# Rows of reciprocal norms: issued by ScalarE and spread over the partitions in one transfer

## The chip, the cores and the metric

The kernel runs on one core of a Trainium2 chip. The metric is the time of one execution on the device in microseconds (us), the median of several runs. The profile is of a single execution, whose span is a few microseconds shorter than the measured time. Everything is in float32.

## What is computed

Attention with normalised queries and keys, followed by a layer that works on a choice of the tokens only:

```
q, k, v: (8, 12, 448, 64);  g_q, g_k: (64)
q_n = q / sqrt(mean(q*q) + 1e-6) * g_q          (k_n likewise)
attn = softmax(q_n @ k_n.T / sqrt(64)) ;  x = attn @ v, as (8, 448, 768)
scores = x @ w_gate ;  the 128 tokens with the highest score of each of the 8 batches:
    out = x + sigmoid(score) * (relu(x @ w1) @ w2)      w1: 768x1024, w2: 1024x768
all other tokens: out = x
```

The part that matters here is the factor 1/rms of each query. It is one number per token and head, and the queries lie in memory transposed: head dimension on the partitions, tokens along the free dimension. So the factor has to be multiplied along the free dimension, with the same row of numbers on each of the 64 partitions of a head.

## The kernel before

The heads are taken in 24 groups of four (three groups to a batch). A group is a tile `qT` and a tile `kT` of 128 partitions (two heads of 64 dimensions) by 2 x 448 tokens, a tile `v`, and two tiles `tok` of 128 partitions by 896 numbers, which hold the same queries and keys with tokens on the partitions. From `tok` the squares are formed on ScalarE (`squares`, L207), their row sums on VectorE (`sum_squares`, L214), and the power -1/2 on GpSimd (L217), giving `rinv` of 128 partitions x 14 numbers.

For the keys, `rinv` is used as it lies, as the scale of the exponential (L298). For the queries it has to change its place. `rows_out` (L225) writes `rinv` to a small tensor `rows` in DRAM, 2 x 896 numbers, so that each pair of heads has its 1/rms in one contiguous row of 3584 bytes. `rows_in` (L233) reads each row back 64 times, onto 64 partitions, giving the tile `bc` (128 x 896). `scale_q` (L245) then multiplies `qT` by `bc` and by the product of both gains on VectorE (L248). Groups 0 and 1 don't take this way: `scale_q_early` spreads their rows by small matmuls.

A group is worked on in 7 units of 64 keys each. `scores` (L281) makes four pairs of matmuls into two PSUM banks (L289) and two exponentials on ScalarE (L298) that write a tile `p`; `values` (L306) multiplies `p` by `v` into two PSUM banks that stay for the whole group (L313); `add_probs` (L321) sums the `p` tiles on VectorE (L335). There are seven `p` buffers and four PSUM banks for scores. Later the sums become denominators (L367, L392, L394), the outputs are turned to tokens on rows (L410) and scaled (L412), and batch by batch the gate, the ranks, the selection by an indirect DMA, and the two layers (L575, L595) follow, in pieces put between the units.

The order is written out by hand: the program runs in manual order, each engine executes its instructions in the order in which the program issues them, and an engine that waits for a semaphore holds everything behind it. A table of slots says when each step is issued; slot u comes with unit u, and 168 units make the attention, s0 = 7n being the first slot of group n. Group n is prepared from slot `first` = max(s0 - 20, 0), or s0 - 17 for n up to 5: squares and sums in slots `first` to `first` + 3, then `rows_out` and `rows_in`; `scale_q` comes in slot max(s0 - 6, `first` + 11). Loads of `tok` are issued 26 slots ahead of s0, `qT` 13, `kT` and `v` 11. The weights w1 and w2 come in 14 parts, one every third slot from slot 16. All plain transfers, loads, rows and the stores of x (L424), are issued by SyncE, on one queue (q1 in the profile). Indirect transfers go by GpSimd (q0), and the queue of ScalarE (q10) carries one small transfer at the start. Each transfer signals its end by a semaphore. The transfers share eight of these, and an issue waits for the last user of the same one.

`bc` has two buffers, `rows` three, `qT` four, `kT` and `v` three each, `tok` six.

Of the kernel before, what the change touches and what calls it, by code (L numbers as in the profile page):

```python
# [68 lines left out]
def fast(  # L69
# [21 lines left out]
    nc = tc.nc  # L91

    B, NP, _, S = loads.src["qT"].shape
    CP = 112
    NJ = S // CP
    D = 64
# [59 lines left out]
    for c in range(2):  # L156
        nc.vector.memset(pick_pair[D * c : D * (c + 1), c : c + 1], 1.0)
    nc.vector.scalar_tensor_tensor(
        out=gg, in0=loads.gcol[:, 0:1], scalar=scale, in1=loads.gcol[:, 1:2], op0=OP.mult, op1=OP.mult
# [43 lines left out]
    def squares(n, i):  # L203
        t = get("tok", n, i)
        sq = sqs[(2 * n + i) % 2]
        for h in [slice(0, 1), slice(1, 2)] if (n, i) == (0, 0) else [slice(0, 2)]:
            nc.scalar.activation(out=sq[:, h, :, 0:D], in_=t[:, h], func=AF.Square, scale=scale)  # L207
        sss[n, i] = norm_pool.tile([128, 2, NI], F32, name="ss", bufs=4)
        return sq

    def sum_squares(n, i, sq):
        ss = sss.pop((n, i))
        for h in [slice(0, 1), slice(1, 2)] if (n, i) == (0, 0) else [slice(0, 2)]:
            nc.vector.tensor_reduce(out=ss[:, h], in_=sq[:, h], axis=AX.X, op=OP.add)  # L214
        rinv = norm_pool.tile([128, 2, NI], F32, name="rinv", bufs=8)
        flat = "p h i -> p (h i)"
        nc.gpsimd.tensor_tensor(  # L217
            out=rinv.rearrange(flat),
            in0=ss.rearrange(flat),
            in1=neg_half.to_broadcast([128, 2 * NI]),  # L220
            op=OP.pow,
        )
        rinvs[n, i] = rinv

    def rows_out(n):  # L225

        rows = dram_pool.tile([2, 2 * S], F32, name="rows", bufs=3)
        nc.sync.dma_start(
            out=rows.rearrange("h (p i) -> p h i", i=NI), in_=rinvs.pop((n, 0))
        )  # L230
        bcs[n] = rows

    def rows_in(n):  # L233

        rows = bcs[n]
        bc = norm_pool.tile([128, 2, S], F32, name="bc")
        for hh in range(2):
            src = rows[hh].rearrange("(c s) -> c s", c=2)
            nc.sync.dma_start(
                out=bc[D * hh : D * (hh + 1)],  # L240
                in_=dataclasses.replace(src, ap=[[0, D]] + [list(x) for x in src.ap]),
            )
        bcs[n] = bc

    def scale_q(n):  # L245
# [388 lines left out]
    def at(slot, fn, *args):  # L634
        todo.setdefault(slot, []).append(lambda: fn(*args))
# [22 lines left out]
    def prepare(n, slot):  # L658
        sq = {}
        for i in range(2):  # L660
            at(slot + 2 * i, lambda i=i: sq.setdefault(i, squares(n, i)))
            at(slot + 2 * i + 1, lambda i=i: sum_squares(n, i, sq.pop(i)))

        at(slot + (7 if n > 2 else 6), rows_out, n)
        at(slot + (10 if n > 5 else 9 if n > 2 else 8), rows_in, n)

    for n in range(1, n_groups):
        s0 = NI * n
        if n > 2:
            at(max(s0 - 26, 4 * (n - 3)), load, "tok", n, 0)  # L670
            at(max(s0 - 26, 4 * (n - 3)), load, "tok", n, 1)
        if n > 1:
            at(max(s0 - 13, 2), load, "qT", n)
            at(max(s0 - 11, 2), load, "kT", n)
            at(max(s0 - 11, 2), load, "v", n)
            first = max(s0 - (20 if n > 5 else 17), 0)
            prepare(n, first)
            at(max(s0 - 6, first + 11), scale_q, n)
# [666 lines left out]
```

## Time and profile before

| | |
|---|---|
| time, median of 3 runs | 531.6 us (530.16 to 532.11) |
| span of the profiled execution | 526.9 us, granted clock 0.994 |
| PE busy | 507.6 us |
| VectorE (DVE) busy | 334.2 us |
| ScalarE (ACT) busy | 278.1 us |
| GpSimd (POOL) busy | 191.8 us |
| DMA | 93.21 MB in 43405 packets |

The busy times are of instructions that compute. Issues of transfers and waits on semaphores are not counted in them; those of SyncE are found under SPq. "Idle before" and "waited for" name the event that released an engine last. A DMA share is the mean over the core's 16 DMA engines, and "us to landing" is counted from the issue to the arrival of the last byte.

### The profile page before, as it was taken

The page shows a single profiled execution, that of the slowest core. Times are in us where ns is not written, and L with a number is a line of the kernel's source. Part 1 is how long each engine was busy: PE and PEld are TensorE (multiplying, and loading weights), DVE is VectorE, ACT ScalarE, POOL GpSimd, SP SyncE. Part 2 cuts the span into 40 slices and gives each one's busy share as a digit, 9 for nine tenths or more (in the row PEclk, how much of TensorE's full clock was granted, in tenths as well). Part 3 has the DMA queues.
Part 4 walks back from the last instruction along what each step waited for, and adds up shares of the span by engine and source line. Part 5 has one row for each costly group of instructions (what it writes and reads, how often), then busy time and mean ns, then how long its engine had stood idle before and what let it go on. Part 6 is the DMA issues. An engine that isn't in the chain of part 4 may idle for free.

```text
span 526.9 us, 11121 instructions
## 1 busy us (share of the span) xinstructions
PE 507.6 (96%) x4482; PEld 298.8 (57%) x4482; DVE 334.2 (63%) x638; ACT 278.1 (53%) x507; POOL 191.8 (36%) x109
## 2 busy tenths in 40 slices
PE   6999997999999999999999999998999999999995
PEld 5544343565744476546654467644664448659694
DVE  4566879579846896658666787467947487336101
ACT  4886873857644845456644585645463474401100
POOL 4956866623512454132712424304621003002102
PEclk9999998999999999999999999999999999999998
DMA  8968779799764297526846396537542231104100
GB/s 304 382 217 291 244 224 345 251 291 340 200 187 161 82 291 232 163 94 192 260 136 183 87 297 211 159 103 223 195 131 71 70 136 31 31 1 143 53 32 35
DMA packets 43405, 93.21 MB, mean 177 GB/s; under 512 B 11059, under 2 KB 23348, under 8 KB 43346
## 3 DMA queue, kind: packets, MB, share of 16 engines
q1 hardware_dynamic: 39938, 86.11, 52.1%
q0 software_dynamic: 3264, 6.31, 3.5%
q8 instruction: 37, 0.61, 0.5%
q14 instruction: 22, 0.18, 0.1%
q10 hardware_dynamic: 144, 0.00, 0.0%
HBM read 74.93 MB, written 25.35 MB: 190 GB/s over the span
## 4 chain that ended last, share of the span: by engine, by line
PE 89%; DVE 4%; DMA 2%; ACT 2%; issue 2%; POOL 0%; DVEq 0%; SPq 0%; ACTq 0%; POOLq 0%
PE sc L289 24%; PE av L313 22%; PE moe_ps L575 13%; PE moe_ps L595 11%; PE sc L595 4%; PE x_ps L410 4%; PE sc L575 4%; PE den_ps L367 3%; DMA bc<-rows 2%; PE denT_ps L392 1%; ACT p L298 1%; DVE sum L335 1%; PE warm_ps L164 1%; DVE ss L214 1%; DVE x L412 1%
## 5 line engine op out<-in xcount | busy, mean ns | idle before, releaser
L298 ACT ACTIVATE p<-sc,rinv 128x448 f32<-128x448 f32 x336 | 186.6, 642 | 106.3 <-PE sc L289 92.5
L217 POOL TENSOR_TENSOR rinv<-ss,neg_half 128x14 f32<-128x14 f32 x48 | 128.8, 2689 | 198.3 <-DVE ss L214 170.6
L289 PE MATMUL sc<-qT,kT 64*64 64x448 f32 x1344 | 154.8, 549 | 1.1 <-DVE qT L268 0.4
L313 PE MATMUL av<-p,v 64*64 64x448 f32 x1344 | 147.1, 537 | 0.0
L335 DVE TENSOR_TENSOR sum<-sum,p 128x896 f32<-128x896 f32 x101 | 111.6, 1105 | 7.2 <-ACT p L298 0.9
L313 PEld LDWEIGHTS av<-p,v 64*64 64x64 f32 x1344 | 60.1, 133 | 67.6 <-issue 56.9
L289 PEld LDWEIGHTS sc<-qT,kT 64*64 64x64 f32 x1344 | 54.3, 133 | 70.9 <-issue 47.0
L214 DVE TENSOR_REDUCE ss<-sq 128x14 f32<-128x910 f32 (+1 forms) x49 | 52.4, 1074 | 33.9 <-ACT sq L207 33.9
L575 PE MATMUL moe_ps<-xeT,w 128*128 128x128 f32 x576 | 69.3, 277 | 0.0
L575 PEld LDWEIGHTS moe_ps<-xeT,w 128*128 128x128 f32 x576 | 66.2, 192 | 5.3 <-issue 5.3
L595 PE MATMUL moe_ps<-w,hT 128*128 128x384 f32 x176 | 61.3, 491 | 0.4 <-DVE xe L604 0.3
L412 DVE TENSOR_TENSOR x<-x_ps,rden 112x512 f32<-112x512 f32 x48 | 32.8, 690 | 37.2 <-PE x_ps L410 36.4
L506 POOL DMA_INDIRECT selected<-x,rank x32 | 33.6, 1050 | 47.3 <-DVE x L498 39.3
L207 ACT ACTIVATE sq<-tok 128x896 f32<-128x896 f32 (+1 forms) x49 | 46.4, 951 | 5.7 <-DMA tok<-in_tok_dram 3.7
L595 PEld LDWEIGHTS moe_ps<-w,hT 128*128 128x128 f32 x176 | 31.7, 190 | 22.5 <-issue 2.5
L436 DVE SCALAR_TENSOR_TENSOR prod<-x,wg 112x256 f32<-112x256 f32 x96 | 41.5, 432 | 3.0
L614 POOL DMA_INDIRECT out_dram<-xe,row x10 | 11.6, 1164 | 81.1 <-DVE rden L394 47.3
L410 PE MATMUL x_ps<-ident,xT 128*112 128x128 f32 x192 | 29.5, 279 | 3.3 <-DVE rden L394 3.3
L335 DVE TENSOR_TENSOR sum<-p 128x896 f32<-128x896 f32 x24 | 25.9, 1078 | 5.2 <-ACT p L298 5.2
L604 DVE SCALAR_TENSOR_TENSOR xe<-sc,xe 128x384 f32<-128x384 f32 (+1 forms) x6 | 3.3, 550 | 40.6 <-PE sc L595 40.6
L410 PEld LDWEIGHTS x_ps<-ident,xT 128*112 128x112 f32 x192 | 21.8, 135 | 12.6 <-issue 7.7
L248 DVE SCALAR_TENSOR_TENSOR qT<-qT,gg,bc 128x896 f32<-128x896 f32 x22 | 25.2, 1147 | 5.1 <-DMA bc<-rows 5.1
(71 smaller groups left out, 311.0 us busy)
## 6 DMA issues: line engine op xcount, KB each, us to landing
tok<-in_tok_dram SPq DMA_DIRECT2D x48, 448.0 KB, 6.3
qT<-in_qT_dram SPq DMA_DIRECT2D x24, 448.0 KB, 6.2
kT<-in_kT_dram SPq DMA_DIRECT2D x24, 448.0 KB, 7.0
v<-in_vp_dram SPq DMA_DIRECT2D x24, 448.0 KB, 7.7
out_dram<-x SPq DMA_DIRECT2D x8, 1344.0 KB, 7.8
bc<-rows SPq DMA_DIRECT2D x44, 224.0 KB, 6.4
xe<-selected SPq DMA_DIRECT2D x8, 385.0 KB, 3.1
w<-in_moe_w_dram SPq DMA_DIRECT2D x6, 512.0 KB, 6.4
```

What stands on the lines that cost most here:

```text
L207: nc.scalar.activation(out=sq[:, h, :, 0:D], in_=t[:, h], func=AF.Square, scale=scale)
L214: nc.vector.tensor_reduce(out=ss[:, h], in_=sq[:, h], axis=AX.X, op=OP.add)
L217: nc.gpsimd.tensor_tensor(out=rinv.rearrange(flat), in0=ss.rearrange(flat), in1=neg_half.to_broadcast([128, 2 * NI]), op=OP.pow,)
L289: nc.tensor.matmul(out=scs[hh][D * c : D * (c + 1), 0:S], lhsT=get("kT", n)[r, c, D * i : D * (i + 1)], rhs=get("qT", n)[r, c, :], start=True,
L298: nc.scalar.activation(out=p[:, hh], in_=scs[hh][:, 0:S], func=AF.Exp, scale=rinvs[n, 1][:, hh, i : i + 1],)
L313: nc.tensor.matmul(out=avs[n][c][D * hh : D * (hh + 1), 0:S], lhsT=get("v", n)[r, hh, i, :], rhs=probs[u][r, hh], start=(i == 0), stop=(i ...
L335: nc.vector.tensor_tensor(out=sums[n], in0=probs.pop(u - 1) if begins else sums[n], in1=probs.pop(u), op=OP.add)
L410: nc.tensor.transpose(out=ps[:CP, j, :], in_=t[:, j, :], identity=ident)
L412: nc.vector.tensor_tensor(out=xs[b][:, :, col : col + 128].rearrange("p j (h d) -> p j h d", d=D), in0=ps[:CP].rearrange("p j (h d) -> p j ...
L436: nc.vector.scalar_tensor_tensor(out=prod, in0=xs[b][:, j, cols], scalar=1.0, in1=wg[:, cols], op0=OP.mult, op1=OP.mult, accum_out=gates[b ...
L575: nc.tensor.matmul(out=ps[:, 128 * i : 128 * i + n], lhsT=w1[:, dc, 128 * (f0 + i) : 128 * (f0 + i + 1)], rhs=xeT[:, dc, :n], start=(dc == 0),
L595: nc.tensor.matmul(out=ps[:n, :width], lhsT=hT[:, fc, :n], rhs=w2[:, fc, cols], start=(fc == 0), stop=(fc == NFC - 1),)
```

## The change

`rows_out` and `rows_in` are issued on the queue of ScalarE instead of that of SyncE, so that they don't stand behind loads and stores that wait for their buffers. The spreading, two transfers of 64 partitions each, becomes one of 128 partitions, whose source is read as 2 rows, each 64 times, 896 numbers. And the two steps are put at fixed distances: `rows_out` in slot `first` + 6 and `rows_in` in slot `first` + 8, where they were one slot and one or two slots later for most groups.

```
     def rows_out(n):
         rows = dram_pool.tile([2, 2 * S], F32, name="rows", bufs=3)
-        nc.sync.dma_start(
+        nc.scalar.dma_start(
             out=rows.rearrange("h (p i) -> p h i", i=NI), in_=rinvs.pop((n, 0))
         )
...
         bc = norm_pool.tile([128, 2, S], F32, name="bc")
-        for hh in range(2):
-            src = rows[hh].rearrange("(c s) -> c s", c=2)
-            nc.sync.dma_start(
-                out=bc[D * hh : D * (hh + 1)],
-                in_=dataclasses.replace(src, ap=[[0, D]] + [list(x) for x in src.ap]),
-            )
+        (h_step, _), row = [list(x) for x in rows.ap]
+        nc.scalar.dma_start(
+            out=bc.rearrange("d c s -> d (c s)"),
+            in_=dataclasses.replace(rows[:, :], ap=[[h_step, 2], [0, D], row]),
+        )
...
-        at(slot + (7 if n > 2 else 6), rows_out, n)
-        at(slot + (10 if n > 5 else 9 if n > 2 else 8), rows_in, n)
+        at(slot + 6, rows_out, n)
+        at(slot + 8, rows_in, n)
```

The program's instructions on PE, VectorE and GpSimd stand in the same order as before. The lines of the changed kernel after these functions have numbers lower by one.

## Prediction

> **What bounds the kernel now.** I read the page top down (busy table, slices, chain, DMA issues), then the wait table, the view of the tile `bc`, and a table by stretches of time.
>
> ```profile
> PE 507.6 (96%) x4482; PEld 298.8 (57%) x4482; DVE 334.2 (63%) x638; ACT 278.1 (53%) x507; POOL 191.8 (36%) x109
> DMA  8968779799764297526846396537542231104100
> GB/s 304 382 217 291 244 224 345 251 291 340 200 187 161 82 291 232 163 94 192 260 136 183 87 297 211 159 103 223 195 131 71 70 136 31 31 1 143 53 32 35
> q1 hardware_dynamic: 39938, 86.11, 52.1%
> q10 hardware_dynamic: 144, 0.00, 0.0%
> ```
>
> PE is busy 507.6 of 526.9 us, so all idle time that any change could give back is 19 us, part of it at the start. DMA is the second resource: 8 or 9 tenths through most of the first third, 5 to 6 tenths in the middle, little after 410 us.
>
> ```profile
> PE 89%; DVE 4%; DMA 2%; ACT 2%; issue 2%; POOL 0%; DVEq 0%; SPq 0%; ACTq 0%; POOLq 0%
> bc<-rows SPq DMA_DIRECT2D x44, 224.0 KB, 6.4
> rows<-rinv SPq DMA_DIRECT2D x22, 7.0 KB, 5.4
> ```
>
> The chain is PE; its DMA share is `bc<-rows` alone, one transfer of 7.98 us from 71.35 us. The wait table and the view of tile `bc`:
>
> ```profile
> DVE qT L248 <- DMA bc<-rows: 5.1, 3, 2.5
> SPq L424 <- DMA out_dram<-xe,row: 77.3, 5, 31.2
> SPq L239 <- DMA rows<-rinv: 32.0, 11, 6.2
> L239 SPq DMA_DIRECT2D bc<-rows x44: 450/504/1890, 27.8 to 410.6; - x44
> DMA to landing us min/median/max: 3.3/6.4/10.5
> ```
>
> VectorE waits for a spreading three times, 5.1 us in all. The worst is group 5: SyncE, held by the store of x, issues `bc` at 70.83 us, it lands at about 79.4, and shortly after PE stands 3.3 us before L410 behind VectorE. SyncE's own waits (32.0 us for rows to land) hold nothing but loads. So before, the rows cost some 4 us. By stretches (columns: PE, PEld, DVE, ACT, POOL busy, PEclk, DMA share, GB/s):
>
> ```profile
> 28.00:130.00 102.00, 96.81 (x1002) 47.13 (x998) 76.97 (x145) 72.53 (x134) 59.03 (x31) 0.98 0.86 277
> 130.00:200.00 70.00, 69.56 (x613) 40.43 (x606) 53.73 (x99) 40.02 (x73) 29.23 (x16) 1.00 0.64 192
> 200.00:410.00 210.00, 208.08 (x1785) 119.28 (x1785) 144.39 (x262) 115.05 (x211) 70.92 (x37) 1.00 0.56 169
> ```
>
> Rate divided by share and by 16 is what one DMA engine moves while busy: 277/0.86/16 = 20.1, 192/0.64/16 = 18.8, 169/0.56/16 = 18.9 GB/s. The best slice moved 382 GB/s, 23.9 per engine. I take 22 GB/s for a saturated one.
>
> **What the Trainium skill says.** "DMA: Bandwidth & Descriptors", section "Why a DMA increments its semaphore by 16 and not by 1": a transfer is cut over the largest number k of engines, up to 16, that divides the slowest dimension of both access patterns; on the SyncE and ScalarE queues these are the lowest-numbered ones. Its "Rules for kernel authors" warn of this very form: a leading dimension of c < 16 confines the whole DMA to at most c engines. The trace of before agrees as far as it goes. If every transfer leaves one packet per contiguous run and one more per engine used, q1 should hold tok 48x(128+16), qT and kT 48x(256+16), v 24x144, x 8x(448+16), bc 44x(64+16), xe 8x144, w 14x144, rows 22x(256+16), wg 112+16 and g 1+1: together 39938, the page's number exactly, and the one-partition g fits only with one engine. No transfer with a leading 2 has run. Section "Issuing engines are not separate DMA queues" of the same page: both queues run on the same 16 engines, so moving the issue opens no bandwidth.
>
> **The change part by part.**
> 1. *The shape of the spreading.* Before: two transfers with a source [64 copies][896] and 64 partitions, k = 16, so each engine carries 2 x 4 runs of 3584 B, 28.7 KB a group. After: source [2][64 copies][896], destination 128 partitions. The largest number dividing 2 and 128 is 2. Two engines carry 64 runs each, 229 KB, and fourteen carry none. At 22 GB/s that is 10.4 us against 1.3; with a fixed cost of about 2 us (the page's section "Anatomy of one DMA", stated for GpSimd's path; the least landing of before, 3.3 us with 14.3 KB an engine, speaks for 2 to 3) one alone lands after 12.5 us, where before had 6.4 amid traffic. Bounds: 23.9 GB/s of the best slice gives 9.6 us, the page's ~27 GiB/s an engine ("Specifications") 7.9, the 18.9 of quiet stretches 12.1.
> 2. *What the two engines must carry.* Extra per group 10.4 - 1.3 = 9.1 us, 22 groups in 383 us (27.8 to 410.6), one per 17.4 us: share +0.52. In the three stretches 0.86, 0.64, 0.56 become 1.38, 1.16, 1.08 at the old pace. Shares above 1 can't be: the pace must fall. A saturated engine also does its other work at 22 rather than 19 to 20 GB/s, so I divide the old share by 1.1: 1.30, 1.10, 1.03. Stretching: 102 us x 0.30 = 31, 70 x 0.10 = 7, 210 x 0.03 = 6; together 44 us. Engines never pack without gaps (the next spreading is issued only after the one before was used, about one slot later), for which I add 5% of 382 us on half of the span, 10 us.
> 3. *Latency.* In before `bc` was used 4.2, 8.5, 8.5, 8.6, 9.1 and 10.8 us after its issue for groups 2 to 7, later 9 to 29. The earlier slots give 2 to 5 us more. 12.5 us plus the loads that share the two engines (five of 28.7 KB a group, 1.3 us each) makes 13 to 19, so groups 2 to 7 must stand on VectorE; behind that wait are the sums of p, L412 and the row sums, and PE follows once the seven p buffers are full. This is the same time as in 2 for the most part; I add 4 us for the first two groups.
> 4. *ScalarE issues them.* 22 x 0.42 + 22 x 0.50 (the issue times of these rows on SyncE) = 20 us on an engine that is idle for 47%: hidden, but for about 2 us. The waits come along: an issue of `bc` waits for its rows (5.4 us to land, two slots of some 2.6 us later) and for the last transfer that used the same one of eight completion semaphores, in the new order of instructions often a load just issued by SyncE (tok, qT, w for groups 2 to 6 and qT for 8 and 9). Queued behind are the exponentials L298 and the copies of xT and den; PE waits for the former after two units. Without a stall I would count 22 x 0.5 us, an issue each that PE sees; here it lies under the stall of 2, and I add 3 us.
> 5. *SyncE is relieved* of 66 issues and 32 us of waiting: loads start earlier, none of them ends a chain now: nothing. The stall of group 5 by the store goes: -4 us.
> Instructions of PE, VectorE and GpSimd keep their order.
> Sum: 44 + 10 + 4 + 2 + 3 - 4 = 59 us, hence 531.6 + 59 = 590; I round down to 588, because the later groups have slack in latency.
>
> **The rivals.**
> - *Two engines, but fast* (29 GB/s, 7.9 us): extra 6.6 us a group, share +0.38; with the old share divided by 1.3 the stretches are 1.04, 0.87, 0.81. Only the first overflows (4 us), and groups 2 to 7 stand 2 to 4 us each (16 us): about 552. For it: the page's figure, and traffic is light late. Against: no stretch shows over 23.9 GB/s an engine.
> - *All sixteen engines carry it, ScalarE's waits count*: 22 x 0.5 us, less the 4 us: +7, about 539. For it: "PEld sc L289 <- ACT p L298" already waits 51 times; against: it needs the division to ignore the leading 2.
> - *All sixteen, the wait goes* (the other side): `bc` leaves in its slot whatever SyncE waits for, 5.1 us of VectorE waits and half of PE's stalls go, some small packets fewer: -6, about 526. Against it stands the same.
> - *Hidden anyway*: ScalarE's waits and the saved stall cancel: 531.
>
> **How the numbers follow.** Saturated pair 0.66 (588, spread 560 to 650), fast pair 0.18 (540 to 562), sixteen with waits 0.04, sixteen and freed 0.09, hidden 0.03. Slower takes the first three: 0.88; faster 0.09; same 0.03. Range: below 535 lie about 0.12; above 645, where 18.9 GB/s would lead (+0.62 a group: about +90 us and more with ScalarE's waits), 0.08.
>
> **What would show it.** Queue q10 should hold 144 + 22x(256+16) + 22x(128+k) packets: 8988 for k = 2, 9296 for k = 16; q1 falls to 30434. `bc<-rows` lands after 12 us and more, VectorE's wait for it grows from 5.1 us to tens, and PE falls below 90% busy, the loss mostly before 200 us. The mean DMA share hardly moves, since fourteen engines idle. A landing near 6 us, or 9296 packets, makes the forecast wrong at its first step; 8988 with a time under 550 makes the rate wrong; long ScalarE waits before L298 with `bc` prompt would move the cause to step 4.

## The result, and the profile after

The changed kernel takes 597.9 us (median of 4 runs, 594.96 to 603.12) where the kernel before takes 530.9 us (530.03 to 532.11): a ratio of 1.127, 95% interval 1.118 to 1.136, or 67 us more. The forecast was 588 us, range 535 to 645, with 0.88 on slower. The profiled execution spans 594.7 us. One execution of `lead4_scalar` ran in a slower state of the chip and is left out below.

From the page of the changed kernel: busy times, three rows of slices, two queues.

```profile
PE 528.8 (89%) x4482; PEld 308.4 (52%) x4482; DVE 331.0 (56%) x638; ACT 279.2 (47%) x507; POOL 191.6 (32%) x109
PE   6967397696597999989999999899989999999995
PEclk9987697899598999999999999899999999999998
DMA  8962475868176452865276247344454313102300
q1 hardware_dynamic: 30434, 75.86, 38.7%
q10 hardware_dynamic: 8988, 10.25, 5.2%
```

The queues first: q10 holds 8988 packets, the figure worked out for two engines; sixteen would have left 9296. Then the PE and DMA rows: the first third of the span, which was dense, has holes in both. DMA falls to 1 or 2 tenths in places, because most of the engines wait with everybody else. Last the busy table: the same 4482 matmuls are busy for 528.8 us instead of 507.6. So of the 67.8 us by which the span grew, 21.2 are PE being busy longer and 46.6 are PE standing still. The PEclk row points to the reason for the 21: its digits of 5 to 8 lie in or beside those slices. The last section looks closer.

The table of waits of the changed kernel (total us, times, longest):

```profile
DVE qT L247 <- DMA bc<-rows: 67.2, 9, 17.0
PE sc L288 <- ACT p L297: 28.2, 7, 11.4
ACT sq L207 <- DMA bc<-rows: 14.0, 2, 12.6
PE x_ps L409 <- DVE rden L393: 13.8, 2, 9.1
ACT p L297 <- DMA rows<-rinv: 8.3, 2, 5.0
```

VectorE's wait for the spreading went from 5.1 to 67.2 us, in nine places. Two rows are new in kind: ScalarE stands for `bc` and for `rows`, and it reads neither. It issues the transfers, in order, and PE waits 28.2 us for the exponentials that stand behind. The longest such place, on the time line of ScalarE:

```profile
131.20 0.51 ACTq L238 DMA_DIRECT2D bc<-rows  x1
...
153.37 0.36 ACTq L228 DMA_DIRECT2D rows<-rinv  x1
153.83 0.95 ACT L207 ACTIVATE sq<-tok 128x896 f32<-128x896 f32 x1 [12.60 <-DMA bc<-rows]
```

Here the rows of group 8 are issued only when the spreading of group 7, issued 22 us before, has landed. The rows need nothing from it; the two share a completion semaphore.

The same stretches as before (PE, PEld, DVE, ACT, POOL busy, PEclk, DMA share, GB/s):

```profile
28.00:130.00 102.00, 72.83 (x678) 31.86 (x673) 44.86 (x87) 50.13 (x91) 46.41 (x26) 0.83 0.55 173
130.00:200.00 70.00, 54.65 (x494) 33.14 (x484) 42.33 (x78) 33.28 (x61) 20.18 (x10) 0.88 0.64 211
200.00:410.00 210.00, 203.01 (x1692) 115.13 (x1685) 138.29 (x250) 112.84 (x205) 71.23 (x35) 0.98 0.52 170
```

From 28 to 130 us PE did 678 recorded matmuls where it had done 1002. By the start of each group's `scale_q`, the changed kernel lags by 15 us at group 2, 30 at group 5, 56 at group 9, 59 at group 13 and 68 at the end. Most of the loss is made in the stretch in which loads, weights and spreadings are all under way.

### The profile page after: what moved, and what is told of

Same layout as the page of the kernel before. It is cut to its first block, busy times and chain, and to the rows that moved or that the text cites. A ratio compares the mean times of both kernels' runs of the same rounds, so it can differ in the third digit from the quotient of the medians.

```text
span 594.7 us, 11104 instructions
## 1 busy us (share of the span) xinstructions
PE 528.8 (89%) x4482; PEld 308.4 (52%) x4482; DVE 331.0 (56%) x638; ACT 279.2 (47%) x507; POOL 191.6 (32%) x109
## 3 DMA queue, kind: packets, MB, share of 16 engines
q10 hardware_dynamic: 8988, 10.25, 5.2%
## 4 chain that ended last, share of the span: by engine, by line
PE 49%; DVE 2%; DMA 2%; issue 1%; ACT 1%; POOL 0%; ACTq 0%; POOLq 0%; DVEq 0%
PE sc L288 12%; PE av L312 11%; PE moe_ps L594 8%; PE moe_ps L574 7%; PE sc L594 4%; PE sc L574 3%; PE x_ps L409 2%; DMA rows<-rinv 1%; PE den_ps L366 1%; PE denT_ps L391 1%; ACT p L297 0%; DMA out_dram<-xe,row 0%; DVE x L411 0%; DVE ss L214 0%; PE row_ps L464 0%
## 5 line engine op out<-in xcount | busy, mean ns | idle before, releaser
L288 PE MATMUL sc<-qT,kT 64*64 64x448 f32 x1344 | 168.8, 581 | 38.6 <-ACT p L297 28.2
L312 PE MATMUL av<-p,v 64*64 64x448 f32 x1344 | 155.3, 551 | 0.0
L288 PEld LDWEIGHTS sc<-qT,kT 64*64 64x64 f32 x1344 | 57.3, 139 | 116.8 <-issue 57.9
L334 DVE TENSOR_TENSOR sum<-sum,p 128x896 f32<-128x896 f32 x101 | 109.9, 1088 | 8.5 <-ACT p L297 2.4
L312 PEld LDWEIGHTS av<-p,v 64*64 64x64 f32 x1344 | 66.2, 138 | 69.8 <-issue 58.5
L247 DVE SCALAR_TENSOR_TENSOR qT<-qT,gg,bc 128x896 f32<-128x896 f32 x22 | 25.3, 1149 | 67.2 <-DMA bc<-rows 67.2
L409 PEld LDWEIGHTS x_ps<-ident,xT 128*112 128x112 f32 x192 | 22.1, 136 | 23.2 <-DVE rden L393 14.4
L341 ACT COPY xT<-av 128x448 f32<-128x448 f32 x48 | 23.4, 549 | 9.9 <-PE av L312 9.3
```

The source lines that it names most:

```text
L288: nc.tensor.matmul(out=scs[hh][D * c : D * (c + 1), 0:S], lhsT=get("kT", n)[r, c, D * i : D * (i + 1)], rhs=get("qT", n)[r, c, :], start=True,
L312: nc.tensor.matmul(out=avs[n][c][D * hh : D * (hh + 1), 0:S], lhsT=get("v", n)[r, hh, i, :], rhs=probs[u][r, hh], start=(i == 0), stop=(i ...
L334: nc.vector.tensor_tensor(out=sums[n], in0=probs.pop(u - 1) if begins else sums[n], in1=probs.pop(u), op=OP.add)
L409: nc.tensor.transpose(out=ps[:CP, j, :], in_=t[:, j, :], identity=ident)
```

## The experiments

Three things changed at once: the width of the spreading (two engines or sixteen), the issuing engine, and the slots. Theory A, the forecast's: the width costs nearly all (58 us), ScalarE's issues and waits 5, and 4 come back because SyncE is relieved. Rival B: ScalarE's waits cost much. Within A a second question is whether the two engines limit the pace (capacity) or only the arrival (latency).

All ratios are to the kernel before on the same chip, with 95% intervals. "Halves" means the spreading in two transfers of 64 partitions; "new slots" means rows in `first` + 6 and spreading in `first` + 8, as in the change. Code is abridged where it has dots.

**Width back to sixteen, the rest of the change kept** (`halves_scalar`). Against the changed kernel:

```
-        nc.scalar.dma_start(out=bc.rearrange("d c s -> d (c s)"), in_=... [[h_step, 2], [0, D], row] ...)
+        for hh in range(2):
+            nc.scalar.dma_start(out=bc[D * hh : D * (hh + 1)], in_=... [[0, D]] + rows[hh] ...)
```

> The changed kernel, but with the spreading as two transfers of 64 partitions (source led by 64 copies), still on ScalarE's queue and in the new slots. Width theory (a leading 2 confines the transfer to two DMA engines): the loss goes, 526 to 540 us, queue q10 holds 144 + 22x272 + 44x80 = 9648 packets, VectorE waits under 10 us for bc. Rival, ScalarE theory (its waits at the issue hold the exponentials): still 585 to 600 us.

Measured: 552.8 us (549.61 to 554.48), ratio 1.041 [1.037, 1.046]. q10 holds 9648 packets, which is 144 + 22 x 272 + 44 x 80, sixteen engines. So the width is worth 598 - 553 = 45 us; but 22 us remain without it, far more than step 4 allowed. The time lies in neither of the two bands expected: both causes are at work.

**Width alone, on the old queue and slots** (`one_sync`). Against the kernel before:

```
-        for hh in range(2):
-            nc.sync.dma_start(out=bc[D * hh : D * (hh + 1)], in_=... [[0, D]] + rows[hh] ...)
+        nc.sync.dma_start(out=bc.rearrange("d c s -> d (c s)"), in_=... [[h_step, 2], [0, D], row] ...)
```

> The kernel before, SyncE issuing in the old slots, with the single spreading of 2 rows x 64 copies. Width theory: about as slow as the changed kernel or a little slower, since bc leaves one or two slots later, 590 to 615 us; q1 holds 30434 + 22x272 + 22x130 = 39278 packets. ScalarE theory: no change from before, 526 to 536 us.

Measured: 574.4 us (573.66 to 574.66), ratio 1.084 [1.081, 1.087]: +45 us again, from the other side. The time lies below the band of the width theory, which had put the whole loss on it. But the two estimates of the width agree: in total it costs the same on both queues, each with its own slots. PE is busy 520.5 us here, at a granted clock of 0.962.

**Four engines instead of two, on ScalarE** (`lead4_scalar`): halves whose source is read as [0, 4], [0, 16], row.

> The changed kernel with two transfers of 64 partitions whose source is led by 4 (4 x 16 copies), so four engines carry 32 runs each in the place of two with 64. Width theory: landing falls from 15 to 22 us to some 8 to 11, which fits the slots of all but group 2: 535 to 555 us; q10 holds 144 + 22x272 + 44x68 = 9120 packets. ScalarE theory: 585 to 600 us. If it isn't the width but the single transfer or the additional dimension as such: either as halves_scalar or as the changed kernel.

Measured: 574.7 us (three executions, 570.38 to 576.68), ratio 1.083 [1.077, 1.089]. q10 holds 9120 packets, so each half ran on four engines, but the time is a miss: 22 us above the sixteen on the same queue and slots, 23 below the two. Bytes per engine halve and about half of the cost stays. The working of step 2 doesn't give that: four engines would carry 115 KB a group in 5.2 us in the place of 1.3, a share of +0.22, and with the old shares divided by 1.1 the stretches come to 1.00, 0.80 and 0.73, with nothing to stretch. Either the arrival counts too, or ScalarE's queue makes it worse; the same lead on SyncE, which would tell, wasn't run.

**The spreading by itself** (`spread_alone`), led by 2, 4, 8 and 64 copies, alone and beside five loads as a group has.

> The spreading by itself: a small kernel of its own that leaves out the attention and all else; it spreads the same two rows of 3584 bytes onto 128 partitions, four times each with a leading 2, 4, 8 and 64, one after the other, then three times with a leading 2 and with 64 beside five loads. Width theory, at 22 GB/s an engine and 2 us fixed: 12.5, 7.2, 4.6 and 3.3 us from issue to use in the quiet part; beside loads 14 to 18 us with 2, 5 to 7 with 64. If the division ignores the leading dimension: all four alike, 3 to 5 us.

The time line of VectorE; the bracket is its wait from the previous sum to the arrival. The rows are leads of 2, 4, 8 and 64 alone, and a lead of 2 beside loads:

```profile
32.44 1.09 DVE L50 TENSOR_TENSOR acc<-acc,bc 128x896 f32<-128x896 f32 x1 [11.65 <-DMA bc<-rows]
...
81.12 1.09 DVE L50 TENSOR_TENSOR acc<-acc,bc 128x896 f32<-128x896 f32 x1 [8.51 <-DMA bc<-rows]
...
107.84 1.09 DVE L50 TENSOR_TENSOR acc<-acc,bc 128x896 f32<-128x896 f32 x1 [5.91 <-DMA bc<-rows]
...
128.60 1.09 DVE L50 TENSOR_TENSOR acc<-acc,bc 128x896 f32<-128x896 f32 x1 [4.19 <-DMA bc<-rows]
...
162.38 1.09 DVE L59 TENSOR_TENSOR acc<-acc,bc 128x896 f32<-128x896 f32 x1 [12.97 <-DMA bc<-rows]
```

A stretch in which one transfer with a lead of 2 is alone (DVE and POOL busy, PEclk, DMA share, GB/s):

```profile
21.00:32.00 11.00, 0.00 (x0) 0.00 (x0) 1.00 0.11 42
```

The share of 0.11 fits two engines of sixteen, which would be 0.125 if they were never idle.

Alone the narrow form arrives after 11.3 to 11.7 us, leads of 4 and 8 after some 8.5 and 5.9, the wide one after 4.2 to 4.6; expected were 12.5, 7.2, 4.6 and 3.3. An engine carries 64, 32 or 16 runs of 3584 bytes with leads of 2, 4 and 8: 3.1 us for 32 runs more is 37 GB/s, 2.6 us for 16 more is 22. (The two leads differ by one more issue in the first comparison, so 37 is too high.) In the last row of the first table the 12.97 us follow 5.6 us of sums over the loads: from the moment the buffer was free, some 18.5 us. Beside loads the wide form took 7.5 and 6.8 us.

**Are the two engines a limit of pace or of arrival?** (`one_sync_early`): one narrow transfer on SyncE, new slots, and groups prepared up to three slots sooner.

```
-            first = max(s0 - (20 if n > 5 else 17), 0)
+            first = max(s0 - (20 if n > 3 else 19 if n > 2 else 17), 0)
```

> The single narrow spreading on SyncE as in one_sync, but groups 3 to 5 are prepared two or three slots earlier and all groups use the new slots, so bc leaves 3 to 5 slots earlier against the same scale_q from group 3 on, except group 2. Latency theory (the two engines have time enough, the landing of 15 to 20 us just misses its use in groups 2 to 9): the loss of 45 us falls by half or more, 545 to 558 us, VectorE's wait under 35 us. Capacity theory (the two engines are full until the weights are in): within 8 us of one_sync, 566 to 582 us.

Measured: 575.3 us (574.01 to 576.61), ratio 1.084 [1.081, 1.088], no gain at all. Waits, `one_sync` first and `one_sync_early` second:

```profile
DVE qT L247 <- DMA bc<-rows: 60.6, 9, 10.5
SPq L238 <- DMA rows<-rinv: 52.8, 16, 10.8
```

```profile
DVE qT L247 <- DMA bc<-rows: 37.3, 8, 10.7
SPq L238 <- DMA rows<-rinv: 162.4, 22, 11.6
```

VectorE waits 23 us less, SyncE 110 us more, and the end is the same. The earlier slots do bring a lead over `one_sync`, 12 us at `scale_q` of group 4 (72.63 for 84.93 us), but at group 10 it is gone (211.57 for 211.04). Between the two, `scale_q` comes every 23.2 us ((211.57 - 72.63)/6), against 17.7 before. All engines together moved 195 GB/s in that stretch. As an estimate from this: 4516 KB a group, of which 459 are spreading; a sixteenth of the rest and half of the spreading, 254 + 229 KB, is what each of the two engines carried, 21 GB/s.

So earlier arrival alone bought nothing, which speaks for pace. One other reading is not excluded by this run. SyncE stood longer for rows, with the loads queued behind, and ScalarE waited for `tok` (first `one_sync`, then this kernel):

```profile
ACT sq L207 <- DMA tok<-in_tok_dram: 5.5, 3, 2.8
ACT sq L207 <- DMA tok<-in_tok_dram: 56.6, 15, 8.5
```

Against it stands that on ScalarE's queue, where no load is behind the rows, the width costs as much, and that the rows themselves land late here, after 14.5 us in the median (5.4 before). But with the four engines above unexplained, how the 45 us divide between pace and arrival is not shown.

**Only the slots** (`halves_sync_new_slots`): the kernel before with

```
-        at(slot + (7 if n > 2 else 6), rows_out, n)
-        at(slot + (10 if n > 5 else 9 if n > 2 else 8), rows_in, n)
+        at(slot + 6, rows_out, n)
+        at(slot + 8, rows_in, n)
```

> The kernel before with nothing changed but the slots (rows out at 6, in at 8 for all groups). If the slots alone cost something (SyncE standing before loads while rows land): 533 to 545 us; if SyncE's wait hides behind loads that come early enough: 526 to 534 us.

Measured: 526.6 us (526.2 to 528.87), ratio 0.992 [0.989, 0.994]. This is the fastest kernel of the study, ahead of both. With it the cost of ScalarE's issuing can be read: 552.8 - 526.6 = 26 us.

**ScalarE with the old slots** (`halves_scalar_old_slots`): the kernel before with both `nc.sync` of the rows replaced by `nc.scalar`.

> The run with two halves on ScalarE, in the slots of the kernel before (rows out at 7, in at 10 for most groups, three slots apart in the place of two). Theory now: ScalarE loses its 23 us because an issue of bc stands until its rows have landed, some 6.6 us, with only two or three short instructions between in the bad groups; a third slot between them puts more work there: 529 to 540 us. Rival, the shared completion semaphores (an issue waits for a load of SyncE that last used the same one): no matter of distance, 545 to 560 us. Rival, the issues as such (66 of them before the exponentials): 550 us again.

Measured: 539.9 us (539.66 to 540.3), ratio 1.017 [1.015, 1.020]: 9 us slower than before. From group 6 on these slots put the spreading three slots behind the rows, where the new ones have two. On ScalarE the new slots cost 13 us; on SyncE they gain 4.

**Only the rows by ScalarE** (`rows_scalar_bc_sync`): new slots, `rows_out` on ScalarE, the halves on SyncE.

> ScalarE issues the rows only (in the new slot), SyncE the two halves of the spreading (in the new slot), so that ScalarE never waits for rows to land. Landing theory: the 23 us go, 526 to 536 us, with a chance to beat the kernel before by the few us of group 5. Semaphore theory: half of the waits stay, 535 to 550 us.

Measured: 527.3 us (527.18 to 527.7), ratio 0.994 [0.992, 0.996]. Moving the rows costs nothing measurable over 526.6. So the 26 us hang on the issue of `bc`, which has to wait for the rows. How it does so is seen in `halves_scalar`. The time line of ScalarE (ACTq marks issues):

```profile
78.61 0.44 ACTq L228 DMA_DIRECT2D rows<-rinv  x1
79.03 0.21 ACT L470 ACTIVATE parts<-parts 112x8 f32<-112x8 f32 x1
79.14 0.94 ACT L207 ACTIVATE sq<-tok 128x896 f32<-128x896 f32 x1
79.98 0.33 ACT L375 COPY den<-den_ps 128x224 f32<-128x224 f32 x1
86.10 1.10 ACTq L239 DMA_DIRECT2D bc<-rows  x2
87.25 0.95 ACT L207 ACTIVATE sq<-tok 128x896 f32<-128x896 f32 x1 [6.93 <-issue]
```

and the chain of waits in the same stretch (start, us, what):

```profile
78.61 7.42 DMA rows<-rinv
86.04 0.03 ACTq L239
...
87.25 0.10 ACT sq L207
87.35 0.76 issue
88.11 0.63 ACT p L298
88.73 0.04 issue
88.78 3.78 PE sc L289 x16
```

Between the two issues ScalarE has 1.5 us of work; the rows take 7.4 us to land; ScalarE stands, and PE with it, since the next exponentials are behind. "issue" in the bracket only says that the engine sat at an issue; the chain names the transfer. There are four such places (issues of rows and `bc` at 78.6 and 86.1, 129.3 and 138.2, 319.6 and 326.0, 385.1 and 393.8 us), and the lag behind the kernel before rises at them, to 8, 13, 19 and 25 us. Each comes soon after a store of x and the loads ahead of it went out on SyncE (at 72.3, 124.0, 313.4 and 377.3 us). Not every store does it: two more go out at 193.8 and 253.7 us, and the lag stays at 13.

Two causes are possible for the 26 us: the landing of the rows, or the completion semaphores that an issue shares with older transfers. At the other three places, too, the chain names the rows:

```profile
129.34 8.78 DMA rows<-rinv
319.55 6.40 DMA rows<-rinv
385.13 8.57 DMA rows<-rinv
```

In each of the four, `bc` goes out within 0.1 us of that landing, so no older transfer held it longer. Distance between the two issues is the test by experiment.

**Seven slots apart** (`halves_scalar_far`): rows in slot 5, spreading in slot 12 (10 for groups 3 to 5).

> Two halves on ScalarE again, rows out at slot 5 and bc at slot 12 (10 for groups 3 to 5, group 2 as it was), so that at least 8 exponentials stand between the two on ScalarE for all later groups. Landing theory: what is left of the loss is group 2 and early bc, 528 to 536 us, hardly any ScalarE wait ended by its own issue. Semaphore theory (bc waits for a load or a store of SyncE that used the same one last): distance from its own rows doesn't matter, 540 us or more.

Measured: 549.2 us (548.61 to 550.08), ratio 1.037 [1.033, 1.040]. Its time lies in the semaphores' band, but its waits say otherwise:

```profile
DVE qT L248 <- DMA bc<-rows: 33.3, 7, 8.5
...
DVE qT L248 <- issue: 12.4, 3, 6.1
...
ACT p L298 <- issue: 6.0, 4, 1.6
```

ScalarE's waits at issues before L298 fell from 28.2 to 6.0 us, while VectorE now waits for the spreading, which leaves too late: second halves issued at 78.2 and used at 85.7, 111.2 and 118.5, 134.6 and 142.8 us. The loss had only moved, so the time decides nothing between the two.

**Four slots apart** (`halves_scalar_gap4`), with the spreading only one slot later than in the change:

```
-        at(slot + 6, rows_out, n)
-        at(slot + 8, rows_in, n)
+        at(slot + (5 if n > 2 else 6), rows_out, n)
+        at(slot + (9 if n > 2 else 8), rows_in, n)
```

> Two halves of 64 partitions, rows and spreading by ScalarE, rows in slot 5 (from group 3 on) and the spreading in slot 9: four slots (some 10 us) apart where the 552.8 us kernel has two, and only one slot later in its arrival. If ScalarE's loss of 26 us is its waiting for rows to land (landings of up to 8.7 us), four slots cover it and the time is 527 to 535 us. If it is the waiting for the shared completion semaphores (older loads and spreadings), distance doesn't help and the time stays at 545 to 555 us. Between them (535 to 545): both.

Measured: 531.9 us (530.88 to 533.63), ratio 1.004 [1.002, 1.006]. The landing theory's band. The chain by engine, `halves_scalar` first and then this kernel:

```profile
PE 79%; DMA 9%; POOL 4%; issue 3%; ACT 2%; DVE 1%; ACTq 1%; SPq 0%; POOLq 0%; DVEq 0%
PE sc L289 22%; PE av L313 19%; PE moe_ps L575 12%; PE moe_ps L595 11%; DMA rows<-rinv 6%; PE sc L595 4%; PE sc L575 3%; PE x_ps L410 3%; POOL rinv L217 2%; PE den_ps L367 2%; DMA tok<-in_tok_dram 2%; ACT p L298 1%; PE denT_ps L392 1%; DMA qT<-in_qT_dram 1%; ACTq L239 1%
```

```profile
PE 89%; DVE 4%; ACT 3%; issue 2%; DMA 1%; ACTq 0%; POOL 0%; DVEq 0%; POOLq 0%
```

`rows<-rinv` was 6% of the chain, about 31 us, and is gone from it, though the rows still take up to 7.3 us to land, where a landing is recorded. So some 20 of the 26 us (1.041 - 1.004 of 530.9) were the landing of the rows. For the rest, VectorE waits twice for `bc`, 9.1 us in all, and the shared semaphores do hold ScalarE here, though briefly: twice the second half of `bc` waits for an older load.

```profile
81.34 0.95 ACT L207 ACTIVATE sq<-tok 128x896 f32<-128x896 f32 x1 [2.51 <-DMA w<-in_moe_w_dram]
134.69 0.95 ACT L207 ACTIVATE sq<-tok 128x896 f32<-128x896 f32 x1 [1.42 <-DMA v<-in_vp_dram]
```

What these cost in the end wasn't told apart.

**The spreading issued by GpSimd** (`halves_bc_gpsimd`), rows by ScalarE, new slots.

> Two halves of 64 partitions in the new slots 6 and 8, rows issued by ScalarE, the spreading issued by GpSimd. The waits of the issue (for rows, for the shared semaphore) are the same as with ScalarE. If the 26 us come from what stands behind a waiting issue on ScalarE, that is the exponentials, the time falls to 525 to 532 us here, with the waits now idle time of GpSimd. If the early slots with a separate queue cost by themselves (contention of the transfers, more waits of others), it stays above 540 us. GpSimd's own way of issuing may cost a few us more of its time; POOL is busy a third of the span.

Measured: 544.8 us (544.11 to 545.42), ratio 1.028 [1.025, 1.031]: a miss, on the side of the other theory. But the early slots don't cost by themselves, as two kernels with the new slots at 526.6 and 527.3 us show. GpSimd waits 92.9 us for rows ahead of `bc`, with its own work queued behind, and VectorE waits 11.2 and 6.1 us for groups 2 and 5; the lag is 9 us by group 2 and 10 by group 10, then grows to 15 at the end. The last 5 lie behind the last scatter (L614): from its issue to the end of the span 10.8 us pass (531.5 to 542.3), and 5.3 before (521.6 to 526.9). Why wasn't tested.

**Eight engines** (`lead8_sync_new_slots`): SyncE, new slots, halves whose source is read as [0, 8], [0, 8], row.

> SyncE, two halves, new slots, but the source led by 8 (8 x 8 copies): eight engines carry 16 runs each a group, the other eight none. Capacity theory: 16 in the place of 8 runs are some 1.3 us more a group on the eight engines, which is room they have: 526 to 533 us. If a zero-step leading dimension costs as such, as in the run led by 4: 545 us or more.

Measured: 529.2 us (20 runs, 525.86 to 532.54), ratio 0.999 [0.997, 1.001]. q1 holds 39586 packets, 44 x 8 fewer than before: eight engines. They carry it at under 1% over sixteen (0.999 against 0.992).

## Why the prediction was right, and which terms were not

The direction and nearly the size were right (588 for 598), but two terms of the sum were off, in opposite ways, so that the total came this close is in part luck. With the runs the ledger reads: slots 526.6 - 530.9 = -4, ScalarE 552.8 - 526.6 = +26, width 597.9 - 552.8 = +45; together +67. The forecast had -4, +5 and +58. The first two depend on the order in which they are taken: with the old slots ScalarE costs 9, and the new slots then 13 more. The 26 belong to ScalarE with two slots between rows and spreading.

1. *Shape* (step 1): right. The rule in the Trainium skill's "DMA: Bandwidth & Descriptors", section "Why a DMA increments its semaphore by 16 and not by 1" gave the packets of every form to the unit: 8988, 9120 and 9648 on q10 for two, four and sixteen engines. The landing alone, 12.5 us in the forecast, is 11.3 to 11.7 us.
2. *Capacity* (steps 2 and 3): the sum was 13 us too large. 44 us of stretching and 10 for gaps were forecast, and 4 for latency; the whole width costs 45. The pace of the two engines, an estimated 21 GB/s, is close to the 22 taken, and in `one_sync_early` an earlier issue brought no gain. But the same working gives nothing for four engines, which cost 22 us, so that 44 and 45 agree doesn't confirm it, and the three terms can't be told apart.
3. *ScalarE's issues* (step 4): the term that was mis-sized, 5 us in the forecast and 26 measured with sixteen engines. The text named the mechanism (rows not landed, exponentials behind) but priced it with the median landing of 5.4 us against "two slots of some 2.6 us". What counts is the tail: in the four places after a store of x the rows take 6.4 to 8.8 us, and ScalarE may have only 1.5 us of its own work between the two issues. The other half of the mechanism, the shared semaphores, shows in the changed kernel, where ScalarE stands 12.6 us for an older narrow spreading. The guess that this would "lie under the stall of 2" is also wrong: the two costs add in total (45 for the width on either queue), though the stalls that make them up differ.
4. *SyncE relieved* (step 5): -4 forecast, -4 measured, but by another way: SyncE needn't be relieved, the earlier slots do it alone. PE's wait for the denominators before L410 falls from 3.3 to 1.3 us in the profile of `halves_sync_new_slots`, and at group 5 it gains 2.5 us. The profiled execution (528.9 us) is the slowest of its four, so the rest of the 4 us isn't shown.
5. *The rival "sixteen engines with ScalarE's waits"* at 539 would have been 553, for the same reason as in 3. The section "Issuing engines are not separate DMA queues" says that issuing on several engines saves only sequencer time. The runs agree as far as they go: the rows alone on ScalarE bring nothing (527.3 against 526.6). They add that the issuing engine also takes over the transfer's wait, and that this can cost 26 us.
6. *What would show it*: packets, VectorE's wait of tens of us, PE at 89% and most of the loss before 200 us came as written. The mean DMA share did move: 0.55 instead of 0.86 in the first stretch, since the fourteen other engines had less to bring per us while the pace fell.

## What to carry to other kernels

Look at the slowest dimension of both sides of a transfer before joining two into one: here a leading 2 put 448 KB on two engines and cost 45 us of 531. A pair of transfers where the second needs the first should be issued by an engine with nothing urgent behind, or so far apart that the worst landing near other traffic (here 9 us, not the median of 4 to 5) is covered; two slots cost 26 us on ScalarE and four slots about 6. If a total comes out right, take it apart all the same: here one term was 13 us too high and another 21 too low.

## What was not expected

The stalls cost twice. PE stalled five times for 4.7 to 11.5 us in the first 160 us, the granted clock was 0.83 from 28 to 130 us and 0.88 from there to 200, and the same matmuls were busy 21 us longer: those of `scores` took 581 ns in the mean where they had taken 549. One of the stalls ends at 93.7 us. The stretches before it, after it and a little later (columns as above):

```profile
82.00:87.00 5.00, 5.00 (x60) 2.35 (x56) 1.10 (x1) 4.72 (x10) 2.58 (x1) 1.00 0.76 232
94.00:99.00 5.00, 5.00 (x28) 1.89 (x30) 4.79 (x14) 2.13 (x4) 5.00 (x3) 0.50 0.38 128
101.00:106.00 5.00, 5.00 (x65) 2.27 (x60) 1.39 (x4) 4.12 (x9) 1.15 (x1) 1.00 0.99 322
```

PE is busy throughout in all three, but right after the stall at half the clock, with 28 matmuls in 5 us where there were 60 and 65; those of `scores` (L288) among them take 951 to 1007 ns, against a median of 536 over the whole run. The Trainium skill's "TensorE: Matmul & The Clock Gate", section "Part 1: The HAM clock gate", says that an idle array is put on a slower clock and has to be busy for a while to get it back. This trace agrees, and so do the kernels side by side, each with less PE idle time and a higher clock: the changed kernel 0.948 (66 us idle), `one_sync` 0.962 (52), `halves_scalar` 0.983 (35), `halves_scalar_gap4` 0.996 (19). The forecast counted lost time as idle time only; of the 67.8 us measured, idle time is 46.6.
